# Order of the first layer's feature blocks, and the place of one low part, in a state-space and mixer kernel

## The chip, the cores and the metric

One core of a Trainium2 chip runs the whole program. The metric is device time in microseconds (us), the median of several executions.

## The reference, cut to what matters

```python
h  = x + ssm_conv(layernorm(x))                      # x: 2048 tokens x 512 features
xb = layernorm(h)
g  = gelu(layernorm(xb) @ w1)                        # first layer, 512 x 512
g0 = g[:, 0:128]   taken from the token one before   # shift +1
g1 = g[:, 128:256] taken from the token one behind   # shift -1
g2 = g[:, 256:384] taken from the token two before   # shift +2
g3 = g[:, 384:512] taken from the token two behind   # shift -2
x1 = xb + concat(g0, g1, g2, g3) @ w2                # second layer, 512 x 512
out = h + x1 + gelu(layernorm(x1) @ w3) @ w4         # third and fourth layer, 512 x 1792 x 512
```

## The kernel before

Two phases follow each other. The convolution phase (`conv_phase`) is put in order by a planner; its instructions are the same in both kernels. The mixer phase (`mixer_phase`) is written out by hand: its wrapper `InOrder` keeps the instructions of each engine in the order in which the Python code issues them, so an instruction that waits holds up all that stands behind it on its engine. Engines: PE multiplies matrices, ACT does activations and casts, DVE and POOL do elementwise work, SP issues transfers (POOL and ACT issue some too).

**Tokens.** `h` holds 16 tiles of 128 tokens. Tile j holds the tokens whose number is j modulo 16, so the neighbour of a token lies in the next tile on the same partition, and only at the edges (tiles -2, -1, 16 and 17) in a copy shifted by one partition, the `wrap` tiles that POOL makes. Four tiles are a group q: group 0 is tiles 0 to 3, group 3 is tiles 12 to 15. Group 3 goes first, since tiles 0 and 1 need its last tiles through the wrap copies; then 0, 1 and 2.

**Statistics and root.** `finish(q, early)` and `finish(q, late)` take mean and variance of two tiles each on DVE (BN_STATS, then BN_AGGR); `root([q])` is a chain of twelve tiny DVE instructions that ends with `rn`, from which `norm1(q)` normalises the tiles of the group. `root([2])` is that of the third group, which is normalised last.

**Turning.** The first layer needs features on partitions. Groups 3 and 0 are turned by PE (`turn1`). Groups 1 and 2 are turned by `swap`: DVE transposes 32x32 blocks, and 16 transfers, 8 issued by SP and 8 by POOL, move the blocks to their partitions. Then `parts` makes for each of the four chunks c a high part on ACT (`xt10h` to `xt13h` for group 1) and a low part on DVE, which is the source minus the high part (`xt10l` to `xt13l`). Numbers are carried as high and low part throughout, and each product is three matmuls: high by high, high by low, low by high (`PROD`; the third number of an entry of `seq`, `xi`, is 1 where the low part of the data is read).

**First layer.** `layer1(q, f)` makes feature block f (128 features) of group q: 12 matmuls of 128x512 into one of four PSUM banks. `gelu` reads the bank twice on ACT, once into the high part `h1_q_fh`, once into `gh1_q_f`, and makes the low part `h1_q_fl` on DVE. Before the change the order of the 12 products is re-sorted for blocks (3, 0) and (1, 0), the first of their groups, so that products with a low part stand a little later.

**Second layer.** `layer2(j)` makes tile j: 12 matmuls, three for each feature block: block 0 from tile j-1, block 1 from tile j+1, block 2 from tile j-2, block 3 from tile j+2, in that order. DVE adds the bank to the residual, and takes statistics for tiles 0 to 7; POOL adds to `h`.

**The order around the change** (lines 1422 to 1435): the first layer of group 0 (four blocks, 0 to 3), `finish(2, late)`, `root([2])`, `parts` of group 1, `layer2(0)` and `layer2(1)`, `norm1(2)`, the second swap, the first layer of group 1, `layer2(2)` and `layer2(3)`, `parts` of group 2, `layer2(4)` and `layer2(5)`, the first layer of group 2, `layer2(6)`, and so on. After `layer2(15)` come 14 steps of the third and fourth layer.

In the views of the profile the helper's line, L87, stands for nearly all instructions. Names are shortened: `l` is a bank of the first, second or fourth layer, `h_3h` and `h_3l` are the parts of feature block 3 of whichever group is under way, `gh` the unrounded activation beside them, `xq` a tile of four normalised or turned tiles, `bs`, `mvh`, `ra`, `rb`, `rr` and `rn` the statistics and the root.

Of the kernel before, what the change touches and what calls it, by code (L numbers as in the profile page):

```python
# [11 lines left out]
F32 = mybir.dt.float32  # L12
# [3 lines left out]
ALU = mybir.AluOpType  # L16
# [276 lines left out]
def norms(nc, cst, qs):  # L293

    ra, rb, rr, nb = cst["norm"]
    mv, t = cst["mv"], slice(qs[0] * 4, qs[-1] * 4 + 4)
    return [
        lambda: nc.vector.tensor_scalar(ra[:, 0, t], mv[:, t, 1], EPS, None, ALU.add),
        lambda: nc.vector.tensor_scalar(ra[:, 1, t], mv[:, t, 1], 1.0 + EPS, EPS * EPS, ALU.mult, ALU.add),
        *rsqrt_ops(nc, None, None, rr[:, :, t], ra[:, :, t], rb[:, :, t]),  # L300
        lambda: nc.vector.scalar_tensor_tensor(
            nb[:, :, t], mv[:, t, 0].unsqueeze(1).to_broadcast([128, 2, len(qs) * 4]), -1.0, rr[:, :, t], ALU.mult, ALU.mult),
    ]
# [825 lines left out]
def mixer_phase(ctx, tc, cst, h, out, finish, w3, w4):  # L1129

    nc = InOrder(tc)
# [10 lines left out]
    def slab(name):  # L1142
        return sl.tile([128, 512], F32R, tag="slab", name=name)

    def slot(i):
        return cst["slab"](i)

    def tmp(name):
        return tm.tile([128, 512], F32, tag="g", name=name, bufs=5)
# [7 lines left out]
    def bank(name):  # L1157
        return ps.tile([128, 512], F32, tag="bank", name=name)
# [11 lines left out]
    def gelu(b, name):  # L1170

        hi, lo, g = slab(f"{name}h"), slab(f"{name}l"), tmp(f"g{name}")
        nc.scalar.activation(hi, b, AF.Gelu_apprx_tanh)
        nc.scalar.activation(g, b, AF.Gelu_apprx_tanh)
        nc.vector.tensor_tensor(lo, g, hi.bitcast(F32), ALU.subtract)
        return hi, lo

    PROD = ((0, 0), (0, 1), (1, 0))
    W1, W2 = cst["w1"], cst["w2"]
# [3 lines left out]
    _, _, rr, nb = cst["norm"]  # L1183
# [3 lines left out]
    def root(qs):  # L1187
        for op in norms(nc, cst, qs):
            op()
# [22 lines left out]
    H1, XL, XT = {}, {}, {}  # L1212
# [25 lines left out]
    def parts(src, name, low=nc.vector):  # L1238

        hi, lo = slab(f"{name}h"), slab(f"{name}l")  # L1240
        src = src.rearrange("p a (i t) -> p i a t", i=4)
        nc.scalar.copy(natural(hi), src)
        low.tensor_tensor(natural(lo), src, natural(hi).bitcast(F32), ALU.subtract)
        return hi, lo

    def layer1(q, f):
        b = bank(f"l1_{q}_{f}")
        n = 0
        seq = [(c, wi, xi) for c in range(4) for wi, xi in PROD]
        if (q, f) in ((3, 0), (1, 0)):  # L1250

            seq.sort(key=lambda k: 2 * k[0] + 3 * k[2])
        for c, wi, xi in seq:
            nc.tensor.matmul(b, W1[f][wi][:, c * 128 : c * 128 + 128], XT[q][c][xi], start=(n == 0), stop=(n == 11))
            n += 1
        H1[q, f] = gelu(b, f"h1_{q}_{f}")

        tiles = {0: ((15, 0),), 2: ((14, 1), (15, 2)), 1: ((0, 3),), 3: ((0, 4), (1, 5))}[f]
        for t, i in tiles:
            if t // 4 != q:  # L1260
                continue
            for k in range(2):
                src = H1[q, f][k][:, t % 4 * 128 : t % 4 * 128 + 128]
                dst = wrap[k][i // 4][:, i % 4, :]
                if f in (0, 2):
                    nc.gpsimd.tensor_copy(dst[:, 32:128], src[:, 0:96].bitcast(F32))
                    nc.gpsimd.tensor_copy(dst[:, 1:32], src[:, 96:127].bitcast(F32))
                    nc.gpsimd.tensor_copy(dst[:, 0:1], zero)
                else:
                    nc.gpsimd.tensor_copy(dst[:, 0:96], src[:, 32:128].bitcast(F32))  # L1270
                    nc.gpsimd.tensor_copy(dst[:, 96:127], src[:, 1:32].bitcast(F32))
                    nc.gpsimd.tensor_copy(dst[:, 127:128], zero)
# [3 lines left out]
    def h1_block(f, j, k):  # L1276
        if 0 <= j < 16:
            return H1[j // 4, f][k][:, j % 4 * 128 : j % 4 * 128 + 128]
        return wrap[k][WRAP[f, j] // 4][:, WRAP[f, j] % 4, :]
# [4 lines left out]
    def layer2(j):  # L1284
        q, i = divmod(j, 4)
        b = bank(f"l2_{j}")
        n = 0
        for f, sh in enumerate((-1, 1, -2, 2)):
            for wi, xi in PROD:
                nc.tensor.matmul(b, h1_block(f, j + sh, xi), W2[f][wi], start=(n == 0), stop=(n == 11))  # L1290
                n += 1
        x1 = quarter(X1[q], i)
        nc.vector.scalar_tensor_tensor(x1, h[:, j, :], r1[:, j : j + 1], b, ALU.mult, ALU.add)
        xq[j] = x1
        if j < 8:
            residual(j), stats2(j)

    def residual(j):
        (nc.gpsimd if j < 12 else nc.vector).tensor_tensor(h[:, j, :], h[:, j, :], xq[j], ALU.add)

    def stats2(j):
        q, i = divmod(j, 4)
        if q not in mv2:
            mv2[q] = sm.tile([128, 4, 2], F32, tag="mv2", name=f"mv2_{q}")
        st = sm.tile([128, 6], F32, tag="bst", name=f"st1_{j}")
        nc.vector.bn_stats(st, xq[j])
        nc.vector.bn_aggr(mv2[q][:, i, :], st)
# [16 lines left out]
    def norm2(q):  # L1324
        for op in norm2_ops(q):
            op()
# [6 lines left out]
    def turn2(q, *how):  # L1333

        for c, v in enumerate(swap(X1[q], XQ[{0: 2, 1: 0, 2: 3, 3: 1}[q]], *how)):
            FT[q, c] = v
# [33 lines left out]
    def raw3(s):  # L1370
        f = s % half
        for i in range(2):
            o = (f + i * half) * 128
            nc.sync.dma_start(raw["ab"[i]].rearrange("p (c f) -> p c f", c=4),
                              w3[:, o : o + 128].rearrange("(c p) f -> p c f", p=128))

    def sum3():
        a11, a12, a21, a22 = (raw[n][:, i * 256 : i * 256 + 256] for n in "ab" for i in range(2))
        s1, s2, s3, s4 = (raw["s"][:, i * 256 : i * 256 + 256] for i in range(4))
        nc.gpsimd.tensor_tensor(s1, a21, a22, ALU.add)  # L1380
        nc.gpsimd.tensor_tensor(s3, a11, a21, ALU.subtract)
        nc.gpsimd.tensor_tensor(s2, s1, a11, ALU.subtract)
        nc.gpsimd.tensor_tensor(s4, a12, s2, ALU.subtract)

    def load3(s, low=nc.gpsimd, parts=range(3)):
        ra, a22, sm_ = raw["a"], raw["b"][:, 256:512], raw["s"]
        if s % 2:
            one, four, last = (slot(11), slot(14)), (slots(4, 2), slots(6, 2)), slot(8)
        else:
            one, four, last = (slot(20), W3S[0]), (slots(16, 2), slots(18, 2)), W3S[1]  # L1390
        for i, (src, (hi, lo)) in enumerate(((ra, one), (sm_, four), (a22, (last[:, 0:256], last[:, 256:512])))):
            if i not in parts:
                continue
            nc.scalar.copy(hi, src)
            low.tensor_tensor(lo, src, hi.bitcast(F32), ALU.subtract)
        at_ = lambda w, i: w[:, i * 256 : i * 256 + 256]
        W3[s] = dict(a11=[at_(w, 0) for w in one], a12=[at_(w, 1) for w in one], a22=[at_(last, i) for i in range(2)],
                     **{f"s{i + 1}": [at_(w, i) for w in four] for i in range(4)})

    def raw4(s):  # L1400
        for i in range(2):
            f = s % half + i * half
            nc.sync.dma_start(raw["45"[i]], w4[f * 128 : f * 128 + 128, :])

    def load4(s):
        W4[s] = []
        for i in range(2):
            o, r = (9 + i * 3 if s % 2 else i * 2), raw["45"[i]]
            nc.scalar.copy(slot(o), r)
            nc.gpsimd.tensor_tensor(slot(o + 1), r, slot(o).bitcast(F32), ALU.subtract)  # L1410
            W4[s].append((slot(o), slot(o + 1)))
# [9 lines left out]
    early, late = range(2), range(2, 4)  # L1421
    norm1(3), finish(0, early), turn1(3), gelus(), finish(0, late), root([0]), norm1(0), finish(1, early)
    layer1(3, 0), layer1(3, 1), layer1(3, 2), turn1(0), finish(1, late), root([1]), norm1(1), raw3(0), raw4(0)
    second = swap(XQ[2], XQ[1], (1, 3, 0, 2), (nc.sync, nc.gpsimd))
    layer1(3, 3), finish(2, early), layer1(0, 0), layer1(0, 1), layer1(0, 2), layer1(0, 3), finish(2, late), root([2])
    XT[1] = [parts(v, f"xt1{c}") for c, v in enumerate(second)]
    layer2(0), layer2(1)
    norm1(2), sum3()
    third = swap(XQ[0], XQ[1], queues=(nc.sync, nc.gpsimd))
    layer1(1, 0), layer1(1, 1), layer1(1, 2), layer1(1, 3), load3(0), raw3(1)  # L1430
    layer2(2), layer2(3)
    XT[2] = [parts(v, f"xt2{c}") for c, v in enumerate(third)]
    norm2(0), layer2(4), layer2(5)
    layer1(2, 0), turn2(0), layer1(2, 1), load4(0), raw4(1), layer1(2, 2), sum3(), layer1(2, 3), layer2(6)
    layer2(7), norm2(1)

    def first_splits():
# [116 lines left out]
    for s in range(2 * half):  # L1554
# [27 lines left out]
        late = layer3b(s)  # L1582
# [56 lines left out]
```

## Time and profile before

| | before |
|---|---|
| median of three runs (lowest, highest) | 690.45 us (690.13, 695.13) |
| the profiled execution | 690.62 us |
| its span, first to last instruction | 688.8 us |
| PE clock granted, mean | 0.995 |
| DVE busy | 547.6 us (79%) |
| ACT busy | 408.0 us (59%) |
| POOL busy | 405.5 us (59%) |

The span is the time from the first to the last instruction of the profiled execution; 1.8 us of its time lie around it. A matmul's row has the start and a modelled end. Matmuls overlap, so the time that one takes from the next is read from the distance between two starts: in the second layer the rows of 128x512 that follow each other start 0.22 to 0.24 us apart where nothing is waited for.

### The profile page before, as it was taken

The page shows a single profiled execution, that of the slowest core. Times are in us where ns is not written, and L with a number is a line of the kernel's source. Part 1 is how long each engine was busy: PE and PEld are TensorE (multiplying, and loading weights), DVE is VectorE, ACT ScalarE, POOL GpSimd, SP SyncE. Part 2 cuts the span into 40 slices and gives each one's busy share as a digit, 9 for nine tenths or more (in the row PEclk, how much of TensorE's full clock was granted, in tenths as well). Part 3 has the DMA queues.
Part 4 walks back from the last instruction along what each step waited for, and adds up shares of the span by engine and source line. Part 5 has one row for each costly group of instructions (what it writes and reads, how often), then busy time and mean ns, then how long its engine had stood idle before and what let it go on. Part 6 is the DMA issues. An engine that isn't in the chain of part 4 may idle for free.

```text
span 688.8 us, 16792 instructions
## 1 busy us (share of the span) xinstructions
PE 650.8 (94%) x6806; PEld 506.4 (74%) x6806; DVE 547.6 (79%) x960; ACT 408.0 (59%) x706; POOL 405.5 (59%) x422
## 2 busy tenths in 40 slices
PE   5887989999999997989999999999999999999997
PEld 5884756663677684748788888888888888888885
DVE  5998898999898998989968799766879954454554
ACT  7889878867889875245634455544465543444330
POOL 1889589968999999002676209455635555554210
PEclk9998999999999999999999999999999999999999
DMA  8830554011201133020232311233311342211004
GB/s 220 270 127 2 175 166 110 3 48 32 64 3 49 34 104 100 2 61 2 62 92 50 103 31 32 61 90 105 98 47 38 105 132 62 62 46 47 18 14 122
DMA packets 49266, 51.49 MB, mean 75 GB/s; under 512 B 6437, under 2 KB 33061, under 8 KB 49189
## 3 DMA queue, kind: packets, MB, share of 16 engines
q1 hardware_dynamic: 47524, 47.80, 24.5%
q10 hardware_dynamic: 1152, 1.57, 0.9%
q0 software_dynamic: 512, 1.05, 0.6%
q8 instruction: 53, 0.87, 0.5%
q14 instruction: 25, 0.20, 0.1%
HBM read 35.72 MB, written 8.39 MB: 64 GB/s over the span
## 4 chain that ended last, share of the span: by engine, by line
PE 60%; DVE 15%; ACT 12%; DMA 4%; issue 4%; POOL 3%; SPq 2%; DVEq 0%; ACTq 0%; POOLq 0%
PE l L87 23%; PE acc L87 11%; ACT pt L87 7%; PE bank L87 6%; DVE u L87 4%; DVE at L87 3%; PE l3a L87 3%; PE l3e L87 3%; PE l3g L87 3%; PE l3d L87 3%; PE l3f L87 3%; PE l3b L87 3%; PE l3c L87 3%; DVE cs L87 2%; DMA h<-in_A_u_dram 2%
## 5 line engine op out<-in xcount | busy, mean ns | idle before, releaser
L87 ACT ACTIVATE pt<-pt 128x1056 f32<-128x1056 int32 x64 | 70.0, 1093 | 14.5 <-DVE cs L87 6.6
L87 POOL TENSOR_TENSOR pt<-p,s 128x512 int32<-128x512 int32 x64 | 71.8, 1137 | 5.0 <-DVE sn L87 3.9
L87 PE MATMUL bank<-at,tbs 128*64 128x128 f32 (+1 forms) x768 | 63.4, 311 | 3.4 <-DVE u L87 1.6
L87 PEld LDWEIGHTS bank<-at,tbs 128*64 128x64 f32 x768 | 44.7, 134 | 20.9 <-ACT at L87 3.0
L87 PEld LDWEIGHTS bank<-ident 128*128 128x128 f32 x418 | 50.4, 198 | 8.3 <-issue 5.1
L87 PE MATMUL bank<-ident 128*128 128x128 f32 x418 | 54.4, 286 | 0.0
L87 PE MATMUL bank<-u,ms 64*128 64x128 f32 x768 | 50.5, 280 | 3.2 <-DVE at L87 1.3
L87 PEld LDWEIGHTS bank<-u,ms 64*128 64x128 f32 x768 | 45.3, 187 | 8.0 <-issue 1.8
L87 POOL TENSOR_TENSOR cs0w<-raw,cs0w 128x512 fp32r<-128x512 f32 x7 | 9.1, 1298 | 58.5 <-ACT cs0w L87 47.4
L87 DVE TENSOR_TENSOR cs<-pt,amx 128x512 f32<-128x512 f32 x64 | 41.0, 679 | 2.5 <-ACT pt L87 1.3
L87 PE MATMUL bank<-cs 128*32 128x64 f32 x1024 | 32.4, 224 | 9.1 <-DVE cs L87 4.8
L87 PEld LDWEIGHTS bank<-cs 128*32 128x32 f32 x1024 | 24.1, 111 | 22.9 <-POOL cs L87 5.9
L87 POOL TENSOR_TENSOR sn1w<-raw,sn1w 128x512 fp32r<-128x512 f32 x7 | 9.5, 1360 | 53.2 <-ACT sn1w L87 42.8
L87 DVE TENSOR_TENSOR h<-h,l 128x512 f32<-128x512 f32 x48 | 32.0, 685 | 10.6 <-PE l L87 10.6
L87 DVE TENSOR_TENSOR u<-u,l3f 128x512 f32<-128x512 f32 x14 | 9.5, 682 | 36.9 <-PE l3f L87 36.9
L87 ACT COPY at<-bank 128x512 f32<-128x512 f32 x40 | 24.9, 627 | 23.3 <-PE bank L87 23.2
L87 ACT ACTIVATE pt<-pt,halfpi 128x1056 f32<-128x1056 f32 x32 | 38.0, 1189 | 0.5
L87 POOL TENSOR_TENSOR sn<-pt,amp 128x512 f32<-128x512 f32 x30 | 36.8, 1227 | 1.4 <-ACT pt L87 1.1
L87 DVE STREAM_TRANSPOSE at<-bank 128x512 f32<-128x512 f32 (+1 forms) x40 | 35.7, 926 | 1.9 <-PE bank L87 1.9
L87 ACT ACTIVATE u<-u 128x512 f32<-128x512 f32 x56 | 35.4, 633 | 1.8
L87 PE MATMUL bank<-sn 128*32 128x64 f32 x1024 | 31.9, 222 | 2.7 <-DVE sn L87 2.5
L87 POOL TENSOR_TENSOR cs<-pt,amp 128x512 f32<-128x512 f32 x26 | 31.8, 1225 | 3.7 <-PE bank L87 1.2
(1161 smaller groups left out, 2084.3 us busy)
## 6 DMA issues: line engine op xcount, KB each, us to landing
raw<-in_B_w_dram SPq DMA_DIRECT2D x28, 256.0 KB, 2.8
xq<-xq SPq DMA_DIRECT2D x72, 64.0 KB, 2.0
h<-in_A_u_dram SPq DMA_DIRECT2D x32, 128.0 KB, 3.9
h<-in_A_u_dram SPq DMA_DIRECT2D x16, 256.0 KB, 4.2
rawa<-in_B_w_dram SPq DMA_DIRECT2D x14, 256.0 KB, 2.8
rawb<-in_B_w_dram SPq DMA_DIRECT2D x14, 256.0 KB, 2.9
ms<-in_mm_dram SPq DMA_DIRECT2D x4, 768.0 KB, 11.0
out_dram<-h SPq DMA_DIRECT2D x48, 64.0 KB, 1.7
```

Of the source, the lines that this page charges most:

```text
L87: ins = f(*args, **kw)
```

## The change

The four blocks of the first layer are issued in another order in groups 0, 1 and 2. `gelu` hands back the instruction that makes the low part instead of issuing it; `layer1` issues it at once, but for block 2 of group 0, whose low part is issued behind the `parts` of group 1. The re-sorted product order moves with the block that is now the first of group 1, block 3, and there all eight products without a low part of the data now come ahead of the four with one.

```diff
 def gelu(b, name):
-        nc.vector.tensor_tensor(lo, g, hi.bitcast(F32), ALU.subtract)
-        return hi, lo
+        return hi, lo, lambda: nc.vector.tensor_tensor(lo, g, hi.bitcast(F32), ALU.subtract)
-    def layer1(q, f):
+    def layer1(q, f, later=False):
-        if (q, f) in ((3, 0), (1, 0)):
-            seq.sort(key=lambda k: 2 * k[0] + 3 * k[2])
+        if (q, f) in ((3, 0), (1, 3)):
+            seq.sort(key=lambda k: 2 * k[0] + (3 if q == 3 else 8) * k[2])
-        H1[q, f] = gelu(b, f"h1_{q}_{f}")
+        *H1[q, f], low = gelu(b, f"h1_{q}_{f}")
+        if later:
+            return low
+        low()
-    layer1(3, 3), finish(2, early), layer1(0, 0), layer1(0, 1), layer1(0, 2), layer1(0, 3), finish(2, late), root([2])
+    layer1(3, 3), finish(2, early), layer1(0, 3), layer1(0, 1), layer1(0, 0)
+    low = layer1(0, 2, True)
+    finish(2, late), root([2])
     XT[1] = [parts(v, f"xt1{c}") for c, v in enumerate(second)]
+    low()
     layer2(0), layer2(1)
-    layer1(1, 0), layer1(1, 1), layer1(1, 2), layer1(1, 3), load3(0), raw3(1)
+    layer1(1, 3), layer1(1, 1), layer1(1, 0), layer1(1, 2), load3(0), raw3(1)
-    layer1(2, 0), turn2(0), layer1(2, 1), load4(0), raw4(1), layer1(2, 2), sum3(), layer1(2, 3), layer2(6)
+    layer1(2, 1), turn2(0), layer1(2, 0), load4(0), raw4(1), layer1(2, 3), sum3(), layer1(2, 2), layer2(6)
```

On DVE, between the first and the second half of the third group's statistics, four low parts of group 0 (`h_0_0l` is block 0 of group 0) become three, in the new block order:

```order
 L87 BN_AGGR mvh<-bs 128x2 x2
-L87 TENSOR_TENSOR h_0_0l<-gh_0_0_4225,h_0_0h 128x512
-L87 TENSOR_TENSOR h_0_1l<-gh_0_1_4244,h_0_1h 128x512
-L87 TENSOR_TENSOR h_0_2l<-gh_0_2_4269,h_0_2h 128x512
-L87 TENSOR_TENSOR h_0_3l<-gh_0_3_4288,h_0_3h 128x512
+L87 TENSOR_TENSOR h_0_3l<-gh_0_3_4225,h_0_3h 128x512
+L87 TENSOR_TENSOR h_0_1l<-gh_0_1_4256,h_0_1h 128x512
+L87 TENSOR_TENSOR h_0_0l<-gh_0_0_4281,h_0_0h 128x512
 L87 BN_STATS bs<-h 128x6 x2
```

The statistics, the root and the four low parts of `xt1` behind it stand one low part nearer, and the low part of the last block made no longer stands ahead of them; `h_0_2l` now stands behind `xt13l`, ahead of the addition for `layer2(0)`.

On PE, the first block of group 1, which before is block 0 (`l_1_0`) and reads high and low parts by turns:

```order
L87 MATMUL l_1_0_4401<-xt10h,cs0w 128x512 x2
L87 MATMUL l_1_0_4401<-xt11h,cs0w 128x512 x2
L87 MATMUL l_1_0_4401<-xt10l,cs0w 128x512
L87 MATMUL l_1_0_4401<-xt12h,cs0w 128x512 x2
L87 MATMUL l_1_0_4401<-xt11l,cs0w 128x512
L87 MATMUL l_1_0_4401<-xt13h,cs0w 128x512 x2
L87 MATMUL l_1_0_4401<-xt12l,cs0w 128x512
L87 MATMUL l_1_0_4401<-xt13l,cs0w 128x512
```

The same place on PE in the changed kernel, where the first block of group 1 is block 3 (`l_1_3`):

```order
L87 MATMUL l_1_3_4401<-xt10h,sn0w 128x512 x2
L87 MATMUL l_1_3_4401<-xt11h,sn0w 128x512 x2
L87 MATMUL l_1_3_4401<-xt12h,sn0w 128x512 x2
L87 MATMUL l_1_3_4401<-xt13h,sn0w 128x512 x2
L87 MATMUL l_1_3_4401<-xt10l,sn0w 128x512
L87 MATMUL l_1_3_4401<-xt11l,sn0w 128x512
L87 MATMUL l_1_3_4401<-xt12l,sn0w 128x512
L87 MATMUL l_1_3_4401<-xt13l,sn0w 128x512
```

The first low part is read behind eight matmuls instead of four; the last one still comes last.

On DVE, the low parts of group 2, beside the four transposes of `turn2(0)`:

```order
-L87 TENSOR_TENSOR h_2_0l<-gh_2_0_4608,h_2_0h 128x512
+L87 TENSOR_TENSOR h_2_1l<-gh_2_1_4608,h_2_1h 128x512
 L87 STREAM_TRANSPOSE xq_3950<-xq_3951 128x4x4x32 x4
-L87 TENSOR_TENSOR h_2_1l<-gh_2_1_4647,h_2_1h 128x512
-L87 TENSOR_TENSOR h_2_2l<-gh_2_2_4672,h_2_2h 128x512
-L87 TENSOR_TENSOR h_2_3l<-gh_2_3_4695,h_2_3h 128x512
+L87 TENSOR_TENSOR h_2_0l<-gh_2_0_4647,h_2_0h 128x512
+L87 TENSOR_TENSOR h_2_3l<-gh_2_3_4672,h_2_3h 128x512
+L87 TENSOR_TENSOR h_2_2l<-gh_2_2_4695,h_2_2h 128x512
```

The low part of block 3, which `layer2(6)` reads from tile 8, moves from the fourth place to the third, and that of block 2 from the third to the fourth. On POOL the wrap copies of block 3 of group 0 now stand ahead of those of block 1, between the same neighbours.

## The prediction

> **What bounds the kernel now.** I read the page first, then who waited for whom on PE from 300 us on, then the engines' busy times in stretches of the mixer phase.
>
> ```profile
> span 688.8 us, 16792 instructions
> PE 650.8 (94%) x6806; PEld 506.4 (74%) x6806; DVE 547.6 (79%) x960; ACT 408.0 (59%) x706; POOL 405.5 (59%) x422
> ...
> PE l L87 <- DVE xt10l L87: 0.9, 1, 0.9
> ...
> 341.00:372.00 31.00, 31.00 (x138) 25.59 (x137) 24.51 (x48) 16.23 (x29) 23.18 (x25) 1.00 0.21 57
> 372.00:374.00 2.00, 1.96 (x9) 1.33 (x8) 1.17 (x2) 0.08 (x1) 1.92 (x3) 1.00 0.43 108
> 374.00:680.00 306.00, 306.00 (x1350) 252.92 (x1350) 211.33 (x337) 138.45 (x230) 140.42 (x121) 1.00 0.24 65
> ```
>
> The stretches give stretch, length, then busy time and count for PE, its weight loads, DVE, ACT and POOL, then PE's clock, the transfers' share and GB/s. From 374 to 680 us PE has no idle time and a full clock: 306 us for 1350 matmuls, 0.227 us each. This part can only start sooner or later; it can't shrink unless matmuls go, and the change removes none. Only what PE loses between 331 and 374 us can be won, and that is two short stalls. The chain of waits, with start, length and place, shows both.
>
> ```profile
> 317.50 13.63 PE l L87 x60
> ...
> 331.15 0.60 ACT h_3h L87
> ...
> 332.27 0.69 DVE h_3l L87
> 332.96 1.20 DVE bs L87 x2
> ...
> 337.87 0.70 DVE xt10l L87
> ...
> 338.62 32.36 PE l L87 x140
> 371.00 0.60 ACT h_3h L87
> ...
> 372.12 1.11 DVE h_3l L87
> ...
> 373.27 25.23 PE l L87 x110
> ```
>
> Twice the path leaves PE, goes over an activation and a low part of a feature block 3, and comes back. The first time the low part of block 3 of group 0 holds up the statistics and root of the third group, behind which the low parts of `xt1` stand on DVE. The second time the low part of block 3 of group 2 is itself what `layer2(6)` wants. PE's rows at the two places give their size.
>
> ```profile
> 336.22 0.39 PE L87 MATMUL l<-ptw,h_3h 128*128 128x512 f32 x1
> 336.44 0.73 PE L87 MATMUL l<-xt10h,cs0w 128*128 128x512 f32 x2
> ...
> 340.42 0.50 PE L87 MATMUL l<-xt13l,cs0w 128*128 128x512 f32 x1
> 340.76 0.40 PE L87 MATMUL l<-xt10h,cs0w 128*128 128x512 f32 x1
> ...
> 372.84 0.39 PE L87 MATMUL l<-amp0w,h_3h 128*128 128x512 f32 x1
> 373.27 0.50 PE L87 MATMUL l<-amp0w,h_3l 128*128 128x512 f32 x1
> 373.60 0.39 PE L87 MATMUL l<-ptw,h_3h 128*128 128x512 f32 x1
> ```
>
> From the last matmul of `layer2(1)` (336.22) to the first of the second block of group 1 (340.76) are 13 steps, 13 x 0.227 = 2.95 us; it took 4.54, so 1.59 us are lost. From 372.84 to 373.60 are two steps, 0.45 us; it took 0.76, so 0.31 us are lost. Together 1.90 us, 0.3% of the time: no more is there to be won.
>
> **Part one: the root sooner.** DVE's and ACT's rows around the first stall:
>
> ```profile
> 330.47 0.69 DVE L87 TENSOR_TENSOR h_1l<-gh,h_1h 128x512 fp32r<-128x512 f32 x1
> 331.07 0.68 DVE L87 TENSOR_TENSOR h_2l<-gh,h_2h 128x512 fp32r<-128x512 f32 x1
> 332.88 1.28 DVE L87 BATCH_NORM_STATS2 bs<-h 128x6 f32<-128x512 f32 x2
> 337.87 0.69 DVE L87 TENSOR_TENSOR xt10l<-xq,xt10h 128x512 fp32r<-128x512 f32 x1 [0.62 <-ACT xt12h L87]
> 339.68 0.69 DVE L87 TENSOR_TENSOR xt13l<-xq,xt13h 128x512 fp32r<-128x512 f32 x1
> 340.28 0.74 DVE L87 SCALAR_TENSOR_TENSOR xq<-h,rr,l 128x512 f32<-128x512 f32 x1
> ...
> 335.76 0.62 ACT L87 CAST xt10h<-xq 128x512 fp32r<-128x512 f32 x1 [3.53 <-DVE rr L87]
> 337.33 0.61 ACT L87 CAST xt13h<-xq 128x512 fp32r<-128x512 f32 x1
> 337.85 2.93 ACT L87 ACTIVATE xq<-h,rn,rr 128x512 f32<-128x512 f32 x4
> ```
>
> Two low parts follow each other 0.60 us apart (330.47 to 331.07). In the changed kernel the third low part of group 0 is the last ahead of the statistics, so these start at 331.07 + 0.60 = 331.67 instead of 332.88: 1.21 us sooner, 0.60 for the instruction moved away and 0.61 for the idle time and hand-over from ACT that went with the last block. Statistics and root read only `h`; nothing else holds them, so `xt10l` moves to 336.66 and `xt13l` to 338.47. Their high parts are there (335.76 + 0.62 = 336.38, and 337.33 + 0.61 = 337.94). `xt13l` ends at 339.16; PE began on it 0.05 us after its end before, so now at 339.21.
>
> PE must be ready by then. Its first matmul on `xt10h` came 0.06 us after the cast; on `xt13h` that makes 338.00, its second 338.23, and three low products at 0.227 each bring it to 339.13 for the last. So `xt13l` is still what is late, by 0.08 us. With the old product order the last product would have come at the same time; the new one only moves waiting for `xt10l` behind work that is ready, and I price it at nothing (at 0 to 0.1 us, since either way `xt13l` is last). The next block starts at 340.76 - 1.21 = 339.55. **First term: 1.21 us**, bounds 0 (were DVE held by something else) and 1.59 (the whole stall).
>
> The low part put off stands behind `xt13l`: 0.60 us of DVE ahead of the addition for `layer2(0)`, which starts at 340.28 - 1.21 + 0.60 = 339.67, still 0.61 us sooner. Behind it wait POOL's addition to `h` and its eight transfers of the second swap, which so come sooner, not later. ACT's four normalisations stay at 337.85, since they stand behind the cast of `xt13h`. They end at 340.78, so ACT takes up the first block of group 1 some 1.2 us after PE has left it; four banks cover that.
>
> **Part two: what the blocks wait for later.** Rows that carry the covers:
>
> ```profile
> 333.93 0.39 PE L87 MATMUL l<-sn0w,h_0l 128*128 128x512 f32 x1
> 350.34 0.39 PE L87 MATMUL l<-amp0w,h_2h 128*128 128x512 f32 x1
> 362.18 0.39 PE L87 MATMUL l<-xt23l,cs0w 128*128 128x512 f32 x1
> ...
> 359.61 0.68 DVE L87 TENSOR_TENSOR xt23l<-xq,xt23h 128x512 fp32r<-128x512 f32 x1
> 369.40 1.52 DVE L87 TENSOR_TENSOR h_1l<-gh,h_1h 128x512 fp32r<-128x512 f32 x1
> 370.85 1.22 DVE L87 TENSOR_TENSOR h_2l<-gh,h_2h 128x512 fp32r<-128x512 f32 x1
> ...
> 335.64 0.18 POOL L87 CAST wrap<-zero 128x1 fp32r<-128x1 f32 x1
> 369.07 1.30 POOL L87 TENSOR_TENSOR cs1w<-raw,cs0w 128x512 fp32r<-128x512 f32 x1
> ```
>
> Group 0: block 0 is now the third; its low part ends at 331.75 and is first wanted by `layer2(1)` at 333.93, 2.2 us later. The low part put off ends near 339.7 and is first wanted by `layer2(2)`, at 350.34 before: ten microseconds of cover. Group 1: block 3, which `layer2(2)` wants, is now first; block 2, now last, is wanted by `layer2(6)`. No wait arises. Group 2's first block comes 1.21 us sooner and must find its low parts: `xt23l` ends at 360.29 and would be read at 362.18 - 1.21 = 360.97, so it suffices even if it does not move. The wrap copies change places among themselves and are read near the end of the second layer.
>
> In `layer2(6)` the wait was for the fourth low part of group 2, which ended at 373.23. Block 3 is now the third, and the third ended at 370.85 + 1.22 = 372.07. `layer2(6)` wants it at 372.84 + 0.23 - 1.21 = 371.86; it is late only if DVE there moves by less than 0.2 us, and DVE follows PE here, since the additions of the second layer wait for PE. **Second term: 0.31 us**, bounds 0 and 0.31.
>
> A rule bears on the second term. The rows show a low part beside a POOL addition (369.07) taking 1.52 us, against 0.69 where POOL rests. The Trainium skill, SBUF — State Buffer, "Who interferes with whom", says that a DVE instruction with two SBUF inputs and a GpSimd instruction that reads SBUF share a port as an exclusive lock, so that the later one waits for the whole of the other. By that rule two low parts ahead of `layer2(6)` could each wait 1.30 us and take 1.99, 1.24 us more than the rows show for the two together; the third would end at 372.07 + 1.24 - 1.21 = 372.10, late by 0.24, the second term would be about 0 and the time 689.2 us. The rows have 1.52 and 1.22, so I keep them.
>
> **The sum.** 690.62 (the profiled execution, of which 688.8 is span) - 1.21 - 0.31 = 689.10. The median of the runs shown is 0.17 below the profiled execution, so 688.9; I say 689.0.
>
> **The rivals.**
>
> *The root moves and PE doesn't.* The idle 0.62 us ahead of `xt10l` is put down to `xt12h`, which it does not read; it also waits for the swap's transfers. If these set its time, `xt13l` stays at 339.68, PE runs eight high products and then waits until 340.42 all the same, and only 0.31 is won: 690.3. That the change does nothing at its main place would look the same. Against it: ACT read the same tile at 335.76. Chance 0.10.
>
> *The low parts run into POOL.* POOL's last wrap copy ends at 335.82, and `xt10l` now starts at 336.66: the distance shrinks from 2.05 to 0.84 us. Were POOL still at work there, the four low parts would each take 1.52 instead of 0.69, 3.3 us in all; `xt13l` would end at 342.5 instead of 340.37, and the kernel would be slower by 2.1 less 0.3: 692.4. It turns to a loss from the point where two of the four meet POOL (1.7 against 1.21). For it: the rows at 369 us. Against it: the copies are behind POOL's transfer issues, which the change leaves alone, and would have to come 0.84 us late to meet even the first. That the two can block each other at all is also what the rule in the Trainium skill, SBUF — State Buffer, "Who interferes with whom", says of them; the price is that of the rows. Chance 0.04.
>
> *Both terms hold*: 689.0, own range 688.5 to 689.8. Chance 0.83. The other 0.03 is an execution like the 695.13 among the runs shown.
>
> **How the numbers follow.** The low end takes the whole of both stalls (690.45 - 1.90 = 688.55) and 0.3 us for the spread of the two close runs (690.13 and 690.45): 688.2. The high end takes the first rival with the same spread: 690.6. That leaves out the loss and the odd execution, 0.07, and some error of my own. One per cent, 6.9 us, is about what a measurement of this kernel tells from no change; the whole stake is 1.9 us, so within 1% has 0.97, faster 0.01, slower 0.02 for a wait that I don't see.
>
> **What would show it.** Right: BATCH_NORM_STATS2 near 331.7, `xt10l` near 336.7, the second block of group 1 on PE near 339.5, no gap in `layer2(6)`, and PE without idle time from there to the end. Wrong: `xt10l` still near 337.9; a low part of `xt1` longer than 0.7 us; a new gap on PE ahead of group 2's first block or in the third layer, which would mean that what was won was given back.

## The result, and the profile after

The changed kernel takes 689.12 us (median of 22 runs, 688.74 to 690.0) against 690.48 of the kernel before in the same group (22 runs, 690.13 to 695.13). The ratio is 0.9976, 95% interval 0.9969 to 0.9984: 1.36 us less, a quarter of a per cent.

The page's head and who waited for whom on PE from 300 us on, in the changed kernel:

```profile
span 688.1 us, 16792 instructions
PE 651.2 (95%) x6806; PEld 507.6 (74%) x6806; DVE 548.6 (80%) x960; ACT 408.2 (59%) x706; POOL 405.0 (59%) x422
...
PE xt L87 <- ACT h L87: 1.0, 1, 1.0
PE bank L87 <- DVE at L87: 0.8, 1, 0.8
```

The wait for `xt10l` is gone from the list. The span fell only from 688.8 to 688.1, since an execution as a whole is a poor measure here: the first matmul of `layer2(0)` comes at 330.95 us in the profiled execution of the kernel before and at 331.38 in that of the changed one, behind the same matmuls, of which only the last four blocks stand in another order. Distances inside one execution are better rulers, and the rest of the document uses them. **Ruler A** is from the first matmul of `layer2(0)` to the first of the second block of group 1, 36 matmuls or 8.16 us at 0.227 each; it holds the first stall. **Ruler B** is from the same start to the first matmul of the third layer; it holds both. **Ruler C** is from the same start to the last matmul of the kernel; it shows how much of what is won on B is kept. PE's rows of the changed kernel (start, length):

```profile
331.38 0.62 PE L87 MATMUL l<-sn0w,wrap 128*128 128x512 f32 x2
...
336.82 0.62 PE L87 MATMUL l<-xt10h,sn0w 128*128 128x512 f32 x2
337.28 0.64 PE L87 MATMUL l<-xt11h,sn0w 128*128 128x512 f32 x2
337.76 0.63 PE L87 MATMUL l<-xt12h,sn0w 128*128 128x512 f32 x2
338.22 0.63 PE L87 MATMUL l<-xt13h,sn0w 128*128 128x512 f32 x2
338.69 0.39 PE L87 MATMUL l<-xt10l,sn0w 128*128 128x512 f32 x1
338.92 0.40 PE L87 MATMUL l<-xt11l,sn0w 128*128 128x512 f32 x1
339.27 0.50 PE L87 MATMUL l<-xt12l,sn0w 128*128 128x512 f32 x1
339.88 0.50 PE L87 MATMUL l<-xt13l,sn0w 128*128 128x512 f32 x1
340.22 0.40 PE L87 MATMUL l<-xt10h,cs0w 128*128 128x512 f32 x1
...
372.24 0.39 PE L87 MATMUL l<-amp0w,h_3h 128*128 128x512 f32 x1
372.46 0.39 PE L87 MATMUL l<-amp0w,h_3l 128*128 128x512 f32 x1
372.69 0.39 PE L87 MATMUL l<-ptw,h_3h 128*128 128x512 f32 x1
```

Ruler A is 340.22 - 331.38 = 8.84 us, against 340.76 - 330.95 = 9.81 before: 0.97 us won of the 1.65 that were lost there. The eight high products run without a wait in this execution, and `xt13l` is still what comes last. At `layer2(6)` the three rows stand 0.22 and 0.23 us apart: the second stall is gone. Ruler B is 66.02 us against 67.39: 1.37 us.

Ruler C is 351.90 us against 353.05, so 1.15 us are kept: 0.22 us go again behind ruler B, most of it at one place in the fourth layer (`acc` is one of its banks), where PE wants the low part `h_010l` of the third layer's result. In the kernel before:

```profile
413.10 1.29 POOL L87 TENSOR_TENSOR raws<-rawb 128x256 f32<-128x256 f32 x1 [24.23 <-DMA rawb<-in_B_w_dram]
413.10 0.69 DVE L87 TENSOR_TENSOR h_010l<-u,h_010h 128x512 fp32r<-128x512 f32 x1 [0.16 <-ACT u L87]
...
414.00 0.39 PE L87 MATMUL acc<-cs0w,h_010h 128*128 128x512 f32 x1
414.22 0.39 PE L87 MATMUL acc<-cs0w,h_010l 128*128 128x512 f32 x1
414.45 0.39 PE L87 MATMUL acc<-cs1w,h_010h 128*128 128x512 f32 x1
```

In the changed kernel:

```profile
412.02 0.74 POOL L87 TENSOR_TENSOR raws<-rawb 128x256 f32<-128x256 f32 x1 [24.09 <-DVE u L87]
412.15 1.16 DVE L87 TENSOR_TENSOR h_010l<-u,h_010h 128x512 fp32r<-128x512 f32 x1 [0.16 <-ACT u L87]
...
413.07 0.39 PE L87 MATMUL acc<-cs0w,h_010h 128*128 128x512 f32 x1
413.36 0.50 PE L87 MATMUL acc<-cs0w,h_010l 128*128 128x512 f32 x1
413.70 0.39 PE L87 MATMUL acc<-cs1w,h_010h 128*128 128x512 f32 x1
```

Before, POOL's addition and DVE's low part start together, and POOL's takes 1.29 us; after, POOL starts first and takes 0.74 us, DVE's takes 1.16 instead of 0.69, and PE loses 0.18 us. Whether the change moves this is not shown: the same loss stands in e7 and e10, which win nothing on ruler A. Both 1.15 and 1.37 us lie inside the interval of the whole times, which reaches from 1.1 to 2.1 us.

### The profile page after: what moved, and what is told of

Same layout as the page of the kernel before. It is cut to its first block, busy times and chain, and to the rows that moved or that the text cites. A ratio compares the mean times of both kernels' runs of the same rounds, so it can differ in the third digit from the quotient of the medians.

```text
span 688.1 us, 16792 instructions
## 1 busy us (share of the span) xinstructions
PE 651.2 (95%) x6806; PEld 507.6 (74%) x6806; DVE 548.6 (80%) x960; ACT 408.2 (59%) x706; POOL 405.0 (59%) x422
## 4 chain that ended last, share of the span: by engine, by line
PE 58%; DVE 19%; ACT 12%; issue 4%; POOL 3%; DMA 2%; SPq 1%; DVEq 0%; ACTq 0%; POOLq 0%
PE l L87 19%; PE acc L87 11%; PE bank L87 8%; ACT pt L87 7%; DVE u L87 4%; PE l3e L87 3%; PE l3b L87 3%; PE l3c L87 3%; PE l3a L87 3%; PE l3g L87 3%; PE l3f L87 3%; PE l3d L87 3%; DVE at L87 3%; DVE cs L87 3%; DMA h<-in_A_u_dram 2%
```

## The experiments

All runs in one table, in us. "Statistics" is the start of the second half of the third group's BN_STATS after the start of ruler A; "root" is from the first `ra` to the end of `rn`; "gap" is what PE loses ahead of `h_3l` in `layer2(6)`. The last column is the median of the run, with that of the kernel before in the same group.

| run | A | statistics | root | gap | B | C | time (before beside it) |
|---|---|---|---|---|---|---|---|
| before | 9.81 | 1.93 | 2.84 | 0.20 | 67.39 | 353.05 | 690.48 |
| changed | 8.84 | 0.77 | 3.02 | none | 66.02 | 351.90 | 689.12 (690.48) |
| e1 low part at once | 9.84 | 1.95 | 2.85 | none | 67.02 | 352.94 | 689.72 (690.89) |
| e2 old product order | 8.82 | 0.77 | 3.01 | none | 65.97 | 351.94 | 689.60 (690.89) |
| e3 group 2 alone | 9.83 | 1.93 | 2.85 | none | 67.04 | 352.83 | 689.82 (690.89) |
| e4 copies late | 8.61 | 0.80 | 2.26 | none | 65.73 | 351.96 | 689.50 (690.89) |
| e5 one more low part off | 8.65 | 0.20 | 3.40 | 0.39 | 66.30 | 352.08 | 689.71 (690.59) |
| e6 all together | 8.43 | 0.18 | 2.26 | 0.34 | 66.05 | 351.89 | 689.87 (690.59) |
| e7 low part off alone | 9.82 | 1.93 | 2.84 | 0.85 | 68.06 | 354.02 | 691.70 (690.59) |
| e8 before, copies late | 9.25 | 1.93 | 2.27 | 0.27 | 66.86 | 353.08 | 690.59 (690.59) |
| e9 all, low parts behind the swap | 8.43 | 0.20 | 2.27 | none | 65.58 | 351.60 | 689.26 (690.86) |
| e10 low part off alone, behind the swap | 9.80 | 1.92 | 2.83 | 0.27 | 67.46 | 353.42 | 690.34 (690.86) |
| e11 copies late, old product order | 8.48 | 0.77 | 2.27 | none | 65.64 | 351.90 | 688.83 (690.86) |
| e12 changed again | 8.80 | 0.77 | 2.99 | none | 65.98 | 351.91 | 689.61 (690.86) |

The changed kernel's second profiled execution (e12) repeats the rulers within 0.04 us, while its median moved by half a microsecond from one group to another. In 14 profiled executions ruler A's start lies between 329.99 (e4) and 332.37 us (e7).

**e1, the low part at once.** Which of order and postponement brings the first term?

```diff
-    low = layer1(0, 2, True)
+    layer1(0, 2)
-    low()
```

> The changed kernel with the low part of block 2 of group 0 issued at once again; all block orders stay. My theory (the low parts of xt1 are late because of what stands ahead of the root on DVE): the fourth low part again waits for ACT ahead of the statistics, these start 1.2 us later than in the changed kernel, and the first term is gone: about 690.1 us; the gap in layer2(6) stays away. Rival (the order of blocks and products is what brought the first term): about 689.1 us, as the changed kernel.

Ruler A is 9.84 us, as before the change, and the gap at `layer2(6)` stays away. Without the postponement nothing of the first term is left. The time came 0.4 us under the expected 690.1 and can't decide by itself (ratio 0.9992, 0.9983 to 1.0); the ruler leaves no room for the rival.

**e2, the old product order.**

```diff
-            seq.sort(key=lambda k: 2 * k[0] + (3 if q == 3 else 8) * k[2])
+            seq.sort(key=lambda k: 2 * k[0] + 3 * k[2])
```

> The changed kernel with the old order of the twelve products in the first block of group 1 (high and low by turns). My theory: xt13l is last in either order, so the second block of group 1 starts at the same place and the time is 689.1 to 689.2 us. Rival (running all eight high products first is part of the gain): PE waits early for xt10l and doesn't make it up, 0.5 to 1 us more, 689.6 to 690.1 us.

8.82 us: the product order is worth nothing in this kernel, as priced. The median, 689.60, stands at the rival's end of the two expectations, but the changed kernel as it is took 689.61 in a later group (e12); the ruler settles it.

**e3, group 2 alone**, on the kernel before.

```diff
-    layer1(2, 0), turn2(0), layer1(2, 1), load4(0), raw4(1), layer1(2, 2), sum3(), layer1(2, 3), layer2(6)
+    layer1(2, 1), turn2(0), layer1(2, 0), load4(0), raw4(1), layer1(2, 3), sum3(), layer1(2, 2), layer2(6)
```

> The kernel before with only the block order of group 2 changed (1, 0, 3, 2). My theory: the second term alone, 0.31 us: about 690.2 us, no gap in layer2(6), the stall at group 1 as before (two starts 4.5 us apart over 13 steps). Rival (the gap moves to the next reader, since DVE is as late as before): no gain, 690.5 us, with a gap in layer2(7) or layer2(8).

B falls by 0.35 us with A unchanged, and no gap opens elsewhere on B: the second term, alone. On C 0.22 us of it are left, and the whole time doesn't show it (ratio 0.9992, 0.9983 to 1.0001).

**e4, the copies late.** The first term was smaller than forecast, and the root longer.

```diff
+        if q:
+            wraps(q, f)
+
+    def wraps(q, f):
         tiles = {0: ((15, 0),), 2: ((14, 1), (15, 2)), 1: ((0, 3),), 3: ((0, 4), (1, 5))}[f]
...
     layer2(8), turn2(1, (3, 0, 1, 2), (nc.sync, nc.scalar), first_splits)
+    wraps(0, 3), wraps(0, 1)
```

> The changed kernel with POOL's 24 wrap copies of group 0 moved behind the splits that follow layer2(8), so that POOL rests beside the third group's root. My theory (the first term fell 0.2 us short because the copies stretch the tiny instructions of the root, 3.0 us from the first to the end of rn against 2.3 us in the second group's root): 2.3 us again, the second block of group 1 starts some 0.6 us sooner, 688.5 us. Rival (the copies don't matter, the root is as long for another reason): 3.0 us again, 689.1 us. A risk of its own: the copies come late for layer2(14), then a gap on PE there.

The root's first rows on DVE and the copies beside them on POOL, in the changed kernel:

```profile
333.68 0.28 DVE L87 TENSOR_SCALAR ra<-mvh 128x4 f32<-128x4 f32 x2
334.00 0.27 DVE L87 TENSOR_SCALAR rb<-ra 128x8 int32<-128x8 int32 x1
334.31 0.46 DVE L87 TENSOR_SCALAR rr<-rb 128x8 int32<-128x8 int32 x1
334.80 0.45 DVE L87 TENSOR_TENSOR rb<-rr 128x8 f32<-128x8 f32 x1
...
336.53 0.17 DVE L87 SCALAR_TENSOR_TENSOR rn<-mvh,rr 128x8 f32<-128x8 f32 x1
...
334.44 0.41 POOL L87 CAST wrap<-h_3l 128x96 fp32r<-128x96 f32 x2
334.93 0.41 POOL L87 CAST wrap<-h_1h 128x96 fp32r<-128x96 f32 x2
```

The same rows of DVE in e4, with POOL at rest:

```profile
332.32 0.24 DVE L87 TENSOR_SCALAR ra<-mvh 128x4 f32<-128x4 f32 x2
332.59 0.17 DVE L87 TENSOR_SCALAR rb<-ra 128x8 int32<-128x8 int32 x1
332.80 0.17 DVE L87 TENSOR_SCALAR rr<-rb 128x8 int32<-128x8 int32 x1
333.01 0.17 DVE L87 TENSOR_TENSOR rb<-rr 128x8 f32<-128x8 f32 x1
...
334.41 0.17 DVE L87 SCALAR_TENSOR_TENSOR rn<-mvh,rr 128x8 f32<-128x8 f32 x1
```

Single instructions of 0.17 us take up to 0.46 beside the copies, and the root as a whole 3.02 us instead of 2.26. That part of the theory holds. The gain does not: ruler A fell by 0.23 us, not by 0.6, and the waits left on it stand ahead of the high products, 0.11, 0.12, 0.07 and 0.07 us. With the root short, PE waits for ACT's casts. These begin 4.7 to 4.9 us after ruler A's start in every run but the changed kernel's first (4.51), wherever the root is. What they read comes by the transfers of the first swap, and in all 14 executions the first cast begins 0.31 to 0.36 us after the last of these lands. The 0.23 us are not kept either: C is 351.96 us, against 351.90 in the changed kernel. In the five kernels with the copies late (e4, e6, e8, e9, e11), and in no other, PE loses 0.1 to 0.2 us in the third layer, where it first reads `t100h`; what delays it there stays open.

**e5, one more low part off.** Nothing wants the low part of block 3 of group 3 before `layer2(10)`.

```diff
-    layer1(3, 3), finish(2, early), layer1(0, 3), layer1(0, 1), layer1(0, 0)
+    low3 = layer1(3, 3, True)
+    finish(2, early), layer1(0, 3), layer1(0, 1), layer1(0, 0)
-    low()
+    low(), low3()
```

> The changed kernel with the low part of block 3 of group 3, which no tile wants before layer2(10), put off behind xt13l as well, so that one more instruction of 0.6 us leaves the place ahead of the root. Ruler: the time from the first matmul of layer2(0) to the first of the second block of group 1, 9.81 us in the kernel before, 8.84 in the changed one, 8.16 with no wait at all. My theory: DVE is 0.6 us sooner, but then ACT's casts, which wait for the swap's transfers, are what PE waits for, as in the run with the copies moved away (8.61): 8.5 to 8.6 us. Rival (DVE is all that holds PE here): 8.2 us.

A is 8.65 us, near my number: the casts are a second limit. But the root stretched to 3.40 us, since it now met more of the copies, and the gap at `layer2(6)` came back with 0.39 us, so that B is 0.28 us worse than in the changed kernel. I had not expected that.

**e6, all together**: e4, e5 and the old product order of e2 in one kernel.

> All together: the changed kernel, its copies moved away from the root, the low part of block 3 of group 3 put off too, and the old product order (high and low by turns) in the first block of group 1. My theory: the low parts of xt1 are now so early that the casts are the limit, and with high and low by turns PE has a low product to run while it waits for the next cast; only the first cast is waited for, 8.3 us on the ruler, 0.3 us less than in the run with the copies moved away, and from layer2(0) to the first matmul of the third layer 65.4 us against 66.0 in the changed kernel. Rival (the product order never matters): 8.6 us, 65.7.

8.43 us on ruler A, 0.18 less than e4, where 0.3 was expected. B missed its number by 0.65: the gap at `layer2(6)` took 0.44 back with the slow step behind it. e7 shows by accident where that gap comes from; e9 and e10 test it.

**e7, the low part off alone**, on the kernel before, blocks in the old order.

```diff
-    layer1(3, 3), finish(2, early), layer1(0, 0), layer1(0, 1), layer1(0, 2), layer1(0, 3), finish(2, late), root([2])
+    layer1(3, 3), finish(2, early), layer1(0, 0), layer1(0, 1)
+    low = layer1(0, 2, True)
+    layer1(0, 3), finish(2, late), root([2])
     XT[1] = [parts(v, f"xt1{c}") for c, v in enumerate(second)]
+    low()
```

> The kernel before with only the low part of block 2 of group 0 put off; the block order stays 0, 1, 2, 3, so block 3 is still the last ahead of the statistics. My theory: its low part waits for ACT all the same, the statistics start 1.9 us after the first matmul of layer2(0) as before, nothing is won: 9.8 us on the ruler, the time as before. Rival (each instruction taken away ahead of the root is worth its 0.6 us): 9.2 us.

Ruler A is as expected, 9.82 us: order and postponement work only together. But the kernel got slower (ratio 1.0013, 1.0005 to 1.0022), B by 0.67 us, nearly all of it ahead of `h_3l`:

```profile
374.24 0.39 PE L87 MATMUL l<-amp0w,h_3h 128*128 128x512 f32 x1
375.32 0.50 PE L87 MATMUL l<-amp0w,h_3l 128*128 128x512 f32 x1 [0.70 <-DVE h_3l L87]
```

Postponing has a price, then. The low part stands ahead of DVE's addition for `layer2(0)`, which starts 9.94 us after ruler A's start in e7, 9.33 before. POOL's addition to `h`, its weight sums and its eight transfers of the second swap follow that addition, and behind them its low parts of weights and its additions for tiles 2 and 3. The way back to DVE shows in three kernels; first `xt20l` and then POOL's pair of additions, in the kernel before:

```profile
357.33 1.15 DVE L87 TENSOR_TENSOR xt20l<-xq,xt20h 128x512 fp32r<-128x512 f32 x1 [0.96 <-issue]
...
355.40 2.53 POOL L87 TENSOR_TENSOR h<-h,xq 128x512 f32<-128x512 f32 x2
```

in the changed kernel:

```profile
356.73 1.84 DVE L87 TENSOR_TENSOR xt20l<-xq,xt20h 128x512 fp32r<-128x512 f32 x1 [0.96 <-ACT xt23h L87]
...
355.49 2.53 POOL L87 TENSOR_TENSOR h<-h,xq 128x512 f32<-128x512 f32 x2
```

and in e5:

```profile
356.02 2.48 DVE L87 TENSOR_TENSOR xt20l<-xq,xt20h 128x512 fp32r<-128x512 f32 x1 [0.96 <-ACT xt23h L87]
...
355.40 2.53 POOL L87 TENSOR_TENSOR h<-h,xq 128x512 f32<-128x512 f32 x2
```

Wherever it starts, `xt20l` ends 0.55 to 0.57 us after POOL's pair (358.48 and 357.93, 358.57 and 358.02, 358.50 and 357.93), and so it does in all 14 executions. The sooner PE lets DVE begin, the longer the instruction lasts. So group 2's low parts, the root for group 0's second normalisation behind them, and the low parts that `layer2(6)` wants are held by POOL, and POOL's place is set by the addition for `layer2(0)`. The 14 executions bear this out: that addition starts anywhere from 7.88 to 9.94 us after ruler A's start, and the third low part of group 2 ends 31.78 to 31.85 us after it each time.

**e8, the kernel before with the copies late**, the edit of e4 alone.

> The kernel before with only POOL's 24 wrap copies of group 0 moved behind the splits that follow layer2(8). My theory: the copies stretch the root also here, 2.84 us against 2.26 without them; since DVE is what PE waits for in this kernel, all of it comes through: 9.25 us on the ruler, the time 0.55 us less. Rival (the root is shorter only where the statistics come sooner): 2.8 and 9.8 us.

9.25 us and a root of 2.27: as expected to the hundredth, since DVE alone is waited for there. B is 0.53 less. The median did not move (ratio 0.9994, 0.9985 to 1.0002), and ruler C says why: it is 353.08 us against 353.05. All that was won on B is lost again behind it, for the most part 0.20 us at `t100h` and 0.18 at `h_010l`.

**e9 and e10, the low parts behind the swap.** The low parts put off in e6 and in e7 move on, behind DVE's transposes for the second swap.

```diff
-    low(), low3()
     layer2(0), layer2(1)
     norm1(2), sum3()
     third = swap(XQ[0], XQ[1], queues=(nc.sync, nc.gpsimd))
+    low(), low3()
```

(In e10 the moved line is `low()` alone.)

> As the run with all together, but the two low parts put off stand behind the transposes of the second swap instead of ahead of the addition for layer2(0). My theory (the gap at layer2(6) came back there because each low part ahead of that addition makes POOL's additions, the second swap and with it group 2 0.6 us later): the addition starts about 7.9 us after the first matmul of layer2(0) instead of 9.10, the gap at layer2(6) goes, the ruler to the second block of group 1 stays at 8.4 us, and the stretch from layer2(0) to the third layer is 65.5 us against 66.05 there and 66.02 in the changed kernel. Rival (the gap came back because PE is early and DVE has no more to give): 66.0 us again.

> The kernel before with the low part of block 2 of group 0 put off behind the transposes of the second swap, block orders as before. My theory: the addition for layer2(0) is back at 9.3 us, the gap at layer2(6) at 0.2 to 0.3 us instead of 0.85, and the stretch at 67.4 us, as in the kernel before, instead of 68.06. Rival (putting off a low part costs wherever it goes): 68 us.

In e9 the addition starts at 7.88 us, the gap is gone and B is 65.58. In e10 the addition is back at 9.33 and B at 67.46, with the gap at 0.27. Both as my theory has them: what brought the gap back was the place of the low parts ahead of that addition. (On C e10 is still 0.37 us behind the kernel before.)

**e11 and e12.** e11 is e4 with the old product order; e12 is the changed kernel once more.

> The changed kernel with the copies moved away from the root and the old product order in the first block of group 1. My theory: with the root short the product order matters at last: 8.4 us on the ruler against 8.61, no gap at layer2(6), a stretch of 65.55 us against 65.73. Rival (no effect of the order, as with the copies in place): 8.6 and 65.7 us.

> The changed kernel once more, beside the others of this group, to see how far the stretches differ from one profiled execution to the next. All theories: 66.0 us from layer2(0) to the third layer within 0.1 us; a time of 689.1 us, or up to 0.6 more, as the others moved in the last two groups.

With the copies away the product order is worth 0.13 us (8.61 to 8.48), less than the 0.2 I had put down: a low product fills the time until the next cast, as e11's rows show.

```profile
335.77 0.73 PE L87 MATMUL l<-xt10h,sn0w 128*128 128x512 f32 x2
336.34 0.69 PE L87 MATMUL l<-xt11h,sn0w 128*128 128x512 f32 x2
336.86 0.40 PE L87 MATMUL l<-xt10l,sn0w 128*128 128x512 f32 x1
337.09 0.62 PE L87 MATMUL l<-xt12h,sn0w 128*128 128x512 f32 x2
```

e11 and e9 have the shortest stretches, 0.34 and 0.40 us under e12 in the same group. Their ratios to the kernel before are 0.9976 (0.9965 to 0.9986) and 0.998 (0.997 to 0.999), that of e12 is 0.9986 (0.9977 to 0.9995). Rulers A and B put them ahead of the changed kernel. On ruler C e11 is level with it (351.90 against 351.91), and only e9 keeps something, 0.31 us; the whole times overlap too far to confirm that.

## Why the prediction was right, point by point

The forecast was 689.0 us, the median is 689.12. That they lie 0.12 us apart is in part luck, since the same kernel's median was 689.61 in a later group. The forecast saving is the better test: 1.52 us, against 1.36 by the medians, 1.37 on ruler B and 1.15 on ruler C. By the rulers the terms came out as follows.

*The first term, 1.21 us*, measured 0.97 (1.01 in the second execution). The mechanism is the one named: e1 takes the postponement away and the whole term goes, e3 leaves it out and A stays. The size was off by the step "`xt10l` moves to 336.66", which kept the root at the length it had before. DVE's rows of the changed kernel:

```profile
331.55 0.68 DVE L87 TENSOR_TENSOR h_0l<-gh,h_0h 128x512 fp32r<-128x512 f32 x1
332.15 1.28 DVE L87 BATCH_NORM_STATS2 bs<-h 128x6 f32<-128x512 f32 x2
...
337.32 0.69 DVE L87 TENSOR_TENSOR xt10l<-xq,xt10h 128x512 fp32r<-128x512 f32 x1 [0.62 <-ACT xt11h L87]
...
339.13 0.69 DVE L87 TENSOR_TENSOR xt13l<-xq,xt13h 128x512 fp32r<-128x512 f32 x1
339.73 0.69 DVE L87 TENSOR_TENSOR h_2l<-gh,h_2h 128x512 fp32r<-128x512 f32 x1
340.33 0.75 DVE L87 SCALAR_TENSOR_TENSOR xq<-h,rr,l 128x512 f32<-128x512 f32 x1
```

The statistics start 0.77 us after ruler A's start; the forecast (331.67, the start at 330.95) is 0.72. The root moved forward under POOL's copies and grew from 2.84 to 3.02 us. These 0.05 and 0.18 are the shortfall.

*The product order, priced at nothing*, was right in this kernel (e2). It is worth something only once the root is out of the way (e11).

*The second term, 0.31 us*, measured 0.35 alone (e3). That it also held beside the first term was partly luck, for the reason given was wrong. "DVE follows PE here" fails: the third low part of group 2 ended 41.12 us after ruler A's start before and 40.80 after, 0.32 sooner, where PE came 0.97 sooner. PE wanted it at 41.08, so 0.28 us were left. DVE there follows POOL, and POOL the addition for `layer2(0)`, 9.33 before and 8.95 after. The prediction saw that this addition would come sooner, not that its place against PE's decides the second term. In e5 the addition lies at 9.38 with PE as early as 8.65, and the gap is back. The low part in question in the changed kernel:

```profile
370.95 1.23 DVE L87 TENSOR_TENSOR h_3l<-gh,h_3h 128x512 fp32r<-128x512 f32 x1
```

*The shared port.* The rule named there, from the Trainium skill, SBUF — State Buffer, "Who interferes with whom", agrees with the rows of `xt20l`, which wait for the end of POOL's work. It speaks of one instruction; in e5 the wait was for the end of two additions in a row. The estimate made by it for two low parts was too high here: they took 1.53 and 1.23 us, against 1.52 and 1.22 before.

*The rivals.* The transfers did not set the place of `xt10l`: in e8 it came 0.56 us sooner with a root 0.57 us shorter. The idle 0.62 us ahead of it is no wait for them either. In the traces of the kernels before and after, eight semaphore instructions of DVE's own take it up, 0.10 us from one to the next, and it measures 0.62 or 0.63 us in the ten executions whose root ends late. Only in e4, e6, e9 and e11 is it longer (0.94 to 1.51); there the transfers are the next limit, by way of the casts. The low parts did not meet the copies, which end at 335.95 in the changed kernel, with `xt10l` at 337.32; the root did, a smaller loss on the same path that no rival named. The slower side was real all the same: e7, one part of the change, is slower than before by the low part's place on DVE, at a spot where the prediction had found only cover.

*The signs.* Those named for "right" came, but for the last: PE was not without idle time to the end. The wait for `h_010l`, 0.18 us, is small but of the kind that the prediction named as a sign of being wrong. The whole times also tell more than the prediction allowed them, which was one per cent: the interval of the ratio is 0.08% to either side.

Left open: what moves ruler A's start by up to 2.4 us between executions. The traces show where: PE's 200th matmul already starts anywhere from 31.43 to 32.65 us, long before the first instruction that the change moves, and in e7 the clock granted from 220 to 330 us was 0.98, where the other 13 executions have 1.00. That the tiny instructions of the root wait at a port is an inference; shown is that they take their usual time once the copies are elsewhere.

## What to carry to other kernels

An instruction put off on an engine that works in order is paid for by whatever stands behind its new place: follow that chain through the other engines to the next stall, and choose a place behind the instruction that others wait for (e9, e10). When a chain comes sooner, ask which work of a neighbour it will now run beside, as well as which it will no longer wait for. Changes of a quarter of a per cent are read better from distances between the same instructions within one execution than from whole times, but the distance must reach to the end of the kernel: in e8 a gain of 0.53 us on ruler B was gone again 17 us behind its end.

## What the runs showed of the hardware that was not expected

A DVE instruction that adds or subtracts two tiles in SBUF waited for two POOL additions in a row, not for one: `xt20l` took 2.48 us instead of 0.69 in e5. And DVE instructions on 4 to 8 numbers per partition are slowed by POOL's small casts as well, from 0.17 to 0.46 us, TENSOR_SCALAR with a single tile as input among them. An instruction that reads what 16 transfers brought, `xt10l`, starts 0.62 us after the end of the one before it even when nothing it needs is late: eight semaphore instructions, 0.10 us apart, come first.
